# Five score banks as one tile, or as two tiles of two banks and one shared bank, with the exponential in two parts

## The chip, the cores and the metric

The kernel runs on one core of a Trainium2 chip. The engines of that core that matter here are TensorE (PE: matmuls and transposes, results in PSUM), VectorE (DVE: reductions, subtractions), ScalarE (ACT: exponentials and copies out of PSUM), GpSimd (POOL) and SyncE (SP), whose queue issues the DMAs. Each engine works off its own queue in order; semaphores hold an instruction until others are done. PSUM has eight banks of 512 fp32 values per partition. The metric is the device time of one execution in microseconds; less is better. "Before" is the median of three runs.

## What is computed

Attention over queries that are averaged two by two, then two expert layers:

```python
q_pool = q.reshape(B, H, S // factor, factor, D).mean(axis=3)      # 4 x 8 x 576 x 64
scores = scale * np.matmul(q_pool, k.transpose(0, 1, 3, 2))        # 576 x 1152 per head
scores = scores - np.max(scores, axis=-1, keepdims=True)
attn = np.exp(scores)
attn = attn / (np.sum(attn, axis=-1, keepdims=True) + 1e-09)
x = np.matmul(attn, v)                                             # then (B*S, H*D) = (2304, 512)
h = x @ w_in;  g = np.maximum(0.01 * h, h);  x = g @ w_out         # 512 -> 2048 -> 512
h = np.maximum(np.maximum(x @ w1, x @ w2), x @ w3); x = h @ w_out  # 512 -> 768 -> 512
```

## The kernel before

**Tiling.** The work goes by batches (4) and within a batch by pairs of heads (`NP` = 4), so by 16 pairs `n`. A pair's 576 queries per head are cut into tiles of 128 rows: five tiles in phase 0 (two of each head and one mixed tile "m" with 64 rows of each) and four in phase 1. A score tile is 128 queries by 1152 keys, in three chunks (`SC` = 3) of 384 keys (`SN`), each in a PSUM bank of its own. fp32 values are split into a high and a low part, so a chunk takes two matmuls (four for the mixed tile): six (twelve) for the tile.

**A score tile** (`scores`, L271 to L307): the matmuls, named `s` in the profile; the negated row maxima `mx` on DVE (L299 over the two banks that were filled first, L300 over the third, L301 the minimum of both); the exponential on ACT (L304) from all three banks to `p`, with the row sums as a second output. `normalise` (L309) turns a phase's sums into reciprocals.

**Banks.** In the first batch (`n < NP`) the tiles take turns in one PSUM tile of five banks, `five` (L91): one tile has banks 0, 1, 2 and the next 3, 4, 2, and bank 2, which both use, is filled last. The other three banks hold transposes and preparation (two, `ps_m`) and the value product (one). In the later batches there are three score banks, and the expert layers use the two that are freed.

**Order.** `attention` lays out slots, nine per phase. In each slot the probabilities of the current phase are transposed (`pst`, copied to `pt` by ACT at L344; `psf` and the DVE copy at L353 for the mixed tile), every third slot ends with the value matmuls (`pv`), and at given slots the scores of the next phase, the next pair's preparation (`psq`, `psk`, then L248, L213 on ACT and L252, L216 on DVE) and its loads are put in between. The first batch has no expert layer beside it. Instead eight chunks of expert weights are read from their 64-bit form (`wraw`, two buffers), decoded on DVE (L553 to L563), ACT and POOL, and stored. From the second batch on expert layers of the batch before run between the slots (`m`). A scheduler takes this order, the declared dependences and priorities (maxima and exponentials get a high one, `EARLY`) and makes each engine's queue of it; it also sets the semaphore waits.

All matmuls go through one helper, so they have one line, L108, and are told apart by tile.

Of the kernel before, what the change touches and what calls it, by code (L numbers as in the profile page):

```python
# [7 lines left out]
F32 = mybir.dt.float32  # L8
# [4 lines left out]
ACTF = mybir.ActivationFunctionType  # L13
ALU = mybir.AluOpType
AX = mybir.AxisListType
# [7 lines left out]
def kernel(  # L23
# [21 lines left out]
    nc = tc.nc  # L45
    B, H, S, D = q.shape
    T = S // 2
    NP = H // 2
# [7 lines left out]
    SC = 3  # L56
    SN = S // SC
# [16 lines left out]
    rr_p = ctx.enter_context(tc.tile_pool(name="rr", bufs=6))  # L74
# [13 lines left out]
    psum = ExitStack()  # L88
    ctx.callback(psum.close)
    ps_5 = psum.enter_context(tc.tile_pool(name="ps_5", bufs=1, space=bass.MemoryType.PSUM))  # L90
    five = ps_5.tile([128, 5, 512], F32, name="s5")  # L91

    ident = const.tile([128, 128], F32, name="ident")
    ebias = const.tile([128, 1], F32, name="ebias")
# [29 lines left out]
    def matmul(**kwargs):  # L124
        return on_pe(nc.tensor.matmul, **kwargs)
# [9 lines left out]
    def wide_scores():  # L135
        if not ps_w:
            psum.close()
            ps_s = ctx.enter_context(tc.tile_pool(name="ps_s", bufs=1, space=bass.MemoryType.PSUM))
            ps_w["s"] = ps_s.tile([128, SC, 512], F32, name="s")
            ps_w["m"] = ctx.enter_context(tc.tile_pool(name="ps_n", bufs=2, space=bass.MemoryType.PSUM))  # L140
        return ps_w["s"]
# [19 lines left out]
    def q_of(n):  # L161
        return spare if n < NP and n % 2 else qt
# [99 lines left out]
    def tiles_of(ph):  # L262
        if ph == 0:
            return [("a", 0), ("a", 128), ("b", 0), ("b", 128), ("m", X0 - 64)]
        return [(h, c) for h in "ab" for c in range(X0 + 64, T + 64, 128)]

    ptl = {}
    sums = {}
    flat = [0]

    def scores(n, ph, i):  # L271
        kind, c0 = tiles_of(ph)[i]
        parts = {"a": [0], "b": [1], "m": [0, 1]}[kind]
        steps = [(j, part) for j in parts for part in range(2)]
        if n < NP:
            ps = five[:, 2 * flat[0]:2 * flat[0] + SC]
            order = [1, 2, 0] if flat[0] else [0, 1, 2]
            flat[0] = 1 - flat[0]
        else:
            ps = wide_scores()  # L280
            order = [0, 1, 2]
        for c in order:
            for x, (j, part) in enumerate(steps):
                matmul(
                    out=ps[:, c, 0:SN],
                    lhsT=q_of(n)[j, part][:, c0:c0 + 128],
                    rhs=kts[n][j][:, c * SN:(c + 1) * SN],
                    start=(x == 0),
                    stop=(x == len(steps) - 1),
                )  # L290
        mx = st_p.tile([128, 4], F32, tag="st", name="mx")
        p = p_p.tile([128, SC, SN], F32, tag="p", name="p")
        if (n, ph) not in sums:
            sums[n, ph] = rr_p.tile([128, 8], F32, tag="rr", name="sums")
        rs = sums[n, ph]
        with tc.high_priority(offset=EARLY):
            if n < NP:
                first = ps[:, order[0]:order[0] + 2, 0:SN]
                nc.vector.tensor_reduce(out=mx[:, 1:2], in_=first, axis=AX.XY, op=ALU.max, negate=True)  # L299
                nc.vector.tensor_reduce(out=mx[:, 2:3], in_=ps[:, order[2], 0:SN], axis=AX.X, op=ALU.max, negate=True)  # L300
                nc.vector.tensor_reduce(out=mx[:, 0:1], in_=mx[:, 1:3], axis=AX.X, op=ALU.min)  # L301
            else:
                nc.vector.tensor_reduce(out=mx[:, 0:1], in_=ps[:, :, 0:SN], axis=AX.XY, op=ALU.max, negate=True)  # L303
            nc.scalar.activation(  # L304
                out=p, in_=ps[:, :, 0:SN], func=ACTF.Exp, bias=mx[:, 0:1], accum_out=rs[:, i:i + 1]
            )
        ptl[n, ph, i] = p  # L307

    def normalise(n, ph, i):  # L309
        rs = sums[n, ph]  # L310
        c = slice(i, i + 1)
        if n < FREE:
            if i < len(tiles_of(ph)) - 1:
                return
            c = slice(0, i + 1)
        nc.vector.tensor_scalar(out=rs[:, c], in0=rs[:, c], scalar1=1e-9, scalar2=None, op0=ALU.add)
        nc.vector.reciprocal(out=rs[:, c], in_=rs[:, c])
        if n >= FREE or i == 4:
            p = ptl[n, ph, i]
            nc.vector.tensor_scalar(out=p, in0=p, scalar1=rs[:, i:i + 1], scalar2=None, op0=ALU.mult)  # L320
# [91 lines left out]
    def attention():  # L412
        npair = B * NP
        load_pair(0)
        for j in range(2):
            pool_q(0, j, j + 1)
            prep_q(0, j)
            prep_k(0, j)
            if j == 0:
                for i in range(2):  # L420
                    scores(0, 0, i)
                    normalise(0, 0, i)
# [3 lines left out]
        for i in range(2, 5):  # L426
            scores(0, 0, i)
            normalise(0, 0, i)
# [212 lines left out]
    class Main:  # L641
        n = TM
# [11 lines left out]
    class Rest:  # L654
        n = TR_
# [102 lines left out]
    if True:  # L758
        nc.gpsimd.memset(ident, 0.0)
        nc.gpsimd.affine_select(  # L760
            out=ident, in_=ident, pattern=[[-1, 128]], compare_op=ALU.not_equal, fill=1.0, base=0, channel_multiplier=1
# [73 lines left out]
```

## Time and profile before

| | |
|---|---|
| median of three runs | 1422.62 us (1419.65 to 1423.52) |
| the profiled execution | 1429.25 us, span 1427.5 us |
| PE busy | 1284.6 us, 90% of the span |
| DVE, ACT, POOL busy | 714.9, 628.1, 360.3 us |
| chain that ended last | PE 73%, DVE 12%, ACT 5%, DMA 5%, issue 4% |
| first expert matmul | 261.58 us after the start |

The page gives the busy share of each engine in 40 slices, the chain of work that ended last and the costliest groups of instructions. Other views of the same trace are used below: waits (who waited for whom), a timeline (instructions in order of time), groups by shape, and a table of busy time by stage. Times are microseconds from the start of the span unless marked ns. Busy time says how long an engine worked, not whether anything waited for it; that is read from the idle time in square brackets and what ended it.

### The profile page before, as it was taken

Reading aid. Unit: us, or ns where it says so; the run is one execution under the profiler, and the core shown is the slowest. Engines: PE = TensorE matmul, PEld = TensorE weight load, DVE = VectorE, ACT = ScalarE, POOL = GpSimd, SP = SyncE. Lnnn points to the kernel's source line nnn. Section 1 sums busy time; section 2 is a strip of 40 time slices with the busy share of each in tenths; the row PEclk is TensorE's granted clock in tenths of the full one; section 3 lists DMA queues with packets and bytes.
Section 4 is the critical chain, followed back from the end, with each engine's and each line's share of the span. In section 5 each row is a group of like instructions: output and inputs, shape, how many; then the busy total and the mean of one; then the engine's idle time right before and its main releaser. Section 6 shows DMA issues by size and latency. Waiting matters only on the chain.

```text
span 1427.5 us, 19289 instructions
## 1 busy us (share of the span) xinstructions
PE 1284.6 (90%) x7376; PEld 1029.8 (72%) x7376; DVE 714.9 (50%) x1206; ACT 628.1 (44%) x1181; POOL 360.3 (25%) x322
## 2 busy tenths in 40 slices
PE   3767777888988898999999998999999999999998
PEld 3545555666666676867777786777777778888888
DVE  4575444369778868444555544454545421122110
ACT  3556455455555656444444444353545432111111
POOL 1152011245557554212112111010221002223110
PEclk9888899999999999999999999999999999999999
DMA  3357203265565656435443535353533335443343
GB/s 107 82 192 218 53 18 70 64 191 175 191 213 186 208 175 209 155 121 146 131 146 129 148 122 142 129 162 108 168 123 122 106 107 176 133 131 121 118 133 104
DMA packets 88056, 197.51 MB, mean 138 GB/s; under 512 B 11420, under 2 KB 41884, under 8 KB 87964
## 3 DMA queue, kind: packets, MB, share of 16 engines
q1 hardware_dynamic: 87964, 196.28, 44.1%
q8 instruction: 58, 0.95, 0.3%
q14 instruction: 34, 0.28, 0.1%
HBM read 150.99 MB, written 35.13 MB: 130 GB/s over the span
## 4 chain that ended last, share of the span: by engine, by line
PE 73%; DVE 12%; ACT 5%; DMA 5%; issue 4%; POOL 2%; SPq 0%; DVEq 0%; ACTq 0%; POOLq 0%
PE m L108 38%; PE s L108 11%; PE pv L108 10%; PE pst L108 6%; PE o L108 5%; ACT p L304 2%; DVE mx L303 2%; DMA wraw<-in_moe_w_out_dram 2%; DVE wraw L556 2%; DVE mx L299 1%; DVE wmant L553 1%; DMA qraw<-in_q_dram 1%; DVE q L252 1%; POOL wmant L566 1%; DVE pt L353 1%
## 5 line engine op out<-in xcount | busy, mean ns | idle before, releaser
L108 PE MATMUL m<-x,w 128*128 128x512 f32 x1272 | 320.8, 397 | 0.0
L108 PEld LDWEIGHTS m<-x,w 128*128 128x128 f32 x1272 | 231.3, 188 | 55.6 <-issue 13.5
L344 ACT COPY pt<-pst 128x512 f32<-128x512 f32 x288 | 166.5, 586 | 196.0 <-PE pst L108 194.7
L304 ACT ACTIVATE p<-s,mx 128x1152 f32<-128x1152 f32 x144 | 176.3, 1224 | 141.5 <-DVE mx L303 91.6
L108 PE MATMUL s<-kt,q 128*128 128x384 f32 x840 | 191.2, 363 | 43.5 <-ACT p L304 39.3
L303 DVE TENSOR_REDUCE mx<-s 128x1 f32<-128x1152 f32 x108 | 146.3, 1355 | 123.7 <-PE s L108 121.4
L108 PE MATMUL pv<-pt,v 128*64 128x256 f32 (+1 forms) x1152 | 183.6, 459 | 19.0 <-DVE pt L353 16.5
L108 PE MATMUL pst<-ident,p 128*128 128x128 f32 x1152 | 177.4, 279 | 20.3 <-DVE pt L353 8.9
L108 PEld LDWEIGHTS s<-kt,q 128*128 128x128 f32 x840 | 152.0, 199 | 55.7 <-ACT p L304 46.0
L108 PEld LDWEIGHTS pst<-ident,p 128*128 128x128 f32 x1152 | 140.6, 143 | 57.9 <-issue 10.9
L701 POOL TENSOR_TENSOR g<-t,g 128x512 fp32r<-128x512 f32 x64 | 83.8, 1309 | 347.8 <-DVE g L700 347.8
L108 PE MATMUL m<-g,w 128*128 128x512 f32 x624 | 163.0, 400 | 0.0
L108 PEld LDWEIGHTS pv<-pt,v 128*64 128x64 f32 x1152 | 81.6, 151 | 90.2 <-issue 34.1
L108 PEld LDWEIGHTS m<-g,w 128*128 128x128 f32 x624 | 112.0, 188 | 26.7 <-issue 7.2
L699 ACT ACTIVATE t<-m 128x512 f32<-128x512 f32 x80 | 44.3, 555 | 131.6 <-PE m L108 131.6
L108 PE MATMUL m<-x,wsplit 128*128 128x512 f32 x360 | 98.3, 413 | 0.5 <-ACT pt L344 0.4
L700 DVE CAST g<-t 128x512 fp32r<-128x512 f32 x64 | 31.4, 490 | 111.1 <-ACT t L699 110.6
L566 POOL TENSOR_TENSOR wmant<-wraw 128x512 f32<-128x512 f32 x56 | 63.6, 1137 | 91.9 <-DVE wraw L563 83.2
L580 POOL TENSOR_TENSOR wsplit<-wmant,wsplit 128x512 fp32r<-128x512 f32 x56 | 77.0, 1378 | 35.4 <-ACT wsplit L579 34.2
L639 POOL TENSOR_TENSOR y<-t,y 128x512 fp32r<-128x512 f32 x24 | 31.1, 1296 | 201.7 <-ACT y L638 201.7
L108 PEld LDWEIGHTS m<-x,wsplit 128*128 128x128 f32 x360 | 67.1, 195 | 19.6 <-issue 5.7
L729 DVE TENSOR_TENSOR t<-m,t 128x512 f32<-128x512 f32 (+1 forms) x60 | 38.2, 637 | 83.2 <-PE m L108 72.3
(87 smaller groups left out, 1491.9 us busy)
## 6 DMA issues: line engine op xcount, KB each, us to landing
w<-w SPq DMA_DIRECT2D x176, 512.0 KB, 3.4
w<-wsplit SPq DMA_DIRECT2D x56, 512.0 KB, 3.2
wraw<-in_moe_w_out_dram SPq DMA_DIRECT2D x22, 512.0 KB, 5.8
v<-in_v_dram SPq DMA_DIRECT2D x16, 576.0 KB, 3.8
wraw<-in_moe_w_dram SPq DMA_DIRECT2D x18, 512.0 KB, 5.4
qraw<-in_q_dram SPq DMA_DIRECT2D x15, 576.0 KB
kraw<-in_k_dram SPq DMA_DIRECT2D x15, 576.0 KB, 6.8
q<-q SPq DMA_DIRECT2D x52, 160.0 KB, 3.3
```

Of the source, the lines that this page charges most:

```text
L108: mm = f(*args, **kwargs)
L303: nc.vector.tensor_reduce(out=mx[:, 0:1], in_=ps[:, :, 0:SN], axis=AX.XY, op=ALU.max, negate=True)
L304: nc.scalar.activation(out=p, in_=ps[:, :, 0:SN], func=ACTF.Exp, bias=mx[:, 0:1], accum_out=rs[:, i:i + 1])
L344: nc.scalar.copy(out=dst, in_=ps.rearrange("p (j c) -> p j c", j=2))
L556: nc.vector.scalar_tensor_tensor(out=low.bitcast(F32), in0=low.bitcast(U32), scalar=2.0 ** -32, in1=m, op0=ALU.mult, op1=ALU.add)
L566: nc.gpsimd.tensor_tensor(out=mf, in0=low.bitcast(F32), in1=high.bitcast(F32), op=ALU.mult)
L580: nc.gpsimd.tensor_tensor(out=t[:, 1], in0=r, in1=t[:, 0], op=ALU.subtract)
L639: nc.gpsimd.tensor_tensor(out=t[:, 1], in0=src, in1=t[:, 0], op=ALU.subtract)
L699: nc.scalar.activation(out=t, in_=ps[:, 0:k.n], func=ACTF.Prelu, alpha=0.01)
L700: nc.vector.tensor_copy(out=gt[:, 0], in_=t)
L701: nc.gpsimd.tensor_tensor(out=gt[:, 1], in0=t, in1=gt[:, 0], op=ALU.subtract)
L729: nc.vector.tensor_tensor(out=t, in0=ps[:, 0:k.n], in1=t, op=ALU.max)
```

## The change

The tile `five` becomes two tiles of two banks, `s_pair`, and one tile of one bank, `s_mid`. A score tile puts its first two chunks into one of the pairs, in turn, and its third chunk into `s_mid`. The first maximum (L299) is taken over the pair, the second (L300) over `s_mid`. The exponential is two instructions: first the third chunk from `s_mid`, then the two chunks of the pair; each has a sum of its own (columns 8 and up of `sums`, which grows from 8 to 16 columns, and columns 0 and up), and `normalise` adds them with one more DVE instruction per phase. Later batches are as before.

```diff
-    five = ps_5.tile([128, 5, 512], F32, name="s5")
+    s_pair = [ps_5.tile([128, 2, 512], F32, name=f"s2{i}") for i in range(2)]
+    s_mid = ps_5.tile([128, 512], F32, name="s1")
...
         if n < NP:
-            ps = five[:, 2 * flat[0]:2 * flat[0] + SC]
-            order = [1, 2, 0] if flat[0] else [0, 1, 2]
+            two = s_pair[flat[0]]
             flat[0] = 1 - flat[0]
+            banks = [two[:, 0], two[:, 1], s_mid]
         else:
             ps = wide_scores()
-            order = [0, 1, 2]
-        for c in order:
+            banks = [ps[:, c] for c in range(SC)]
+        for c in range(SC):
...
-                    out=ps[:, c, 0:SN],
+                    out=banks[c][:, 0:SN],
...
             if n < NP:
-                first = ps[:, order[0]:order[0] + 2, 0:SN]
-                nc.vector.tensor_reduce(out=mx[:, 1:2], in_=first, axis=AX.XY, op=ALU.max, negate=True)
-                nc.vector.tensor_reduce(out=mx[:, 2:3], in_=ps[:, order[2], 0:SN], axis=AX.X, op=ALU.max, negate=True)
+                nc.vector.tensor_reduce(out=mx[:, 1:2], in_=two[:, :, 0:SN], axis=AX.XY, op=ALU.max, negate=True)
+                nc.vector.tensor_reduce(out=mx[:, 2:3], in_=s_mid[:, 0:SN], axis=AX.X, op=ALU.max, negate=True)
                 nc.vector.tensor_reduce(out=mx[:, 0:1], in_=mx[:, 1:3], axis=AX.X, op=ALU.min)
+                nc.scalar.activation(
+                    out=p[:, 2], in_=s_mid[:, 0:SN], func=ACTF.Exp, bias=mx[:, 0:1], accum_out=rs[:, 8 + i:9 + i]
+                )
+                nc.scalar.activation(
+                    out=p[:, 0:2], in_=two[:, :, 0:SN], func=ACTF.Exp, bias=mx[:, 0:1], accum_out=rs[:, i:i + 1]
+                )
...
+        if n < NP:
+            nc.vector.tensor_tensor(out=rs[:, c], in0=rs[:, c], in1=rs[:, 8:9 + i], op=ALU.add)
```

The scheduler makes other queues of this for the first batch; behind it every engine's order is the same. Three places show what moves. In the rows a tile's name has its number, and in brackets stand the engines or DMA queues that the instruction waits for. `s5_117` is the tile of five banks; `s20_117`, `s21_118` and `s1_119` are the two pairs and the shared bank.

TensorE at the start, the scores of the second and third tile of the program, before:

```order
L108 MATMUL s5_117<-kt0_204,q00_122 128x384 [waits Activation_49]
L108 MATMUL s5_117<-kt0_204,q01_123 128x384
L108 MATMUL s5_117<-kt0_204,q00_122 128x384
L108 MATMUL s5_117<-kt0_204,q01_123 128x384
L108 MATMUL s5_117<-kt0_204,q00_122 128x384
L108 MATMUL s5_117<-kt0_204,q01_123 128x384
L108 MATMUL pst_357<-ident_118,p_244 128x128 [waits DVE_49,PE_49]
L108 MATMUL pst_376<-ident_118,p_244 128x128 [waits DVE_49]
L108 MATMUL s5_117<-kt1_205,q10_124 128x384 [waits Activation_49]
L108 MATMUL s5_117<-kt1_205,q11_125 128x384
```

The wait of the first of six matmuls is for the exponential of the tile before, also at the second tile, whose first bank that exponential doesn't read. All six stand behind it.

TensorE in the first batch, the scores of the third pair's first tiles, while the second pair's values are worked on (a value product, transposes, the spread reciprocals `psr`), after:

```order
L109 MATMUL s20_117<-kt1_803,q10_126 128x384 [waits DMAHW2_49]
L109 MATMUL s20_117<-kt1_803,q11_127 128x384 [waits DMAHW4_49]
L109 MATMUL s20_117<-kt1_803,q10_126 128x384
L109 MATMUL s20_117<-kt1_803,q11_127 128x384
L109 MATMUL psr_1102<-ident_120,mb_1100 128x128 [waits Activation_49,Pool_49]
L109 MATMUL psr_1102<-ident_120,mb_1100 128x128
L109 MATMUL s1_119<-kt1_803,q10_126 128x384 [waits Activation_49]
L109 MATMUL s1_119<-kt1_803,q11_127 128x384
L109 MATMUL s21_118<-kt1_803,q10_126 128x384 [waits Activation_49]
L109 MATMUL s21_118<-kt1_803,q11_127 128x384
L109 MATMUL s21_118<-kt1_803,q10_126 128x384
L109 MATMUL s21_118<-kt1_803,q11_127 128x384
```

The same place before:

```order
L108 MATMUL psr_1075<-ident_118,mb_1073 128x128 [waits Activation_49,Pool_49]
L108 MATMUL psr_1075<-ident_118,mb_1073 128x128
L108 MATMUL s5_117<-kt1_783,q10_124 128x384 [waits DMAHW6_49,Activation_49]
L108 MATMUL s5_117<-kt1_783,q11_125 128x384 [waits DMAHW1_49]
L108 MATMUL s5_117<-kt1_783,q10_124 128x384
L108 MATMUL s5_117<-kt1_783,q11_125 128x384
L108 MATMUL s5_117<-kt1_783,q10_124 128x384
L108 MATMUL s5_117<-kt1_783,q11_125 128x384
```

The pair of a tile now stands ahead of its shared bank by itself, without a wait for ACT or with one for a tile further back, and `s1_119` waits for the first part of the exponential before it.

DVE at the same place, the maxima of four tiles after (L323 is the added sum of `normalise`):

```order
L299 TENSOR_REDUCE mx_1093<-s20_117 128x1 [waits PE_49,Activation_49]
L300 TENSOR_REDUCE mx_1093<-s1_119 128x1 [waits PE_49]
L299 TENSOR_REDUCE mx_1125<-s21_118 128x1 [waits PE_49,Activation_49]
L301 TENSOR_REDUCE mx_1093<-mx_1093 128x1 [waits DVE_49]
L300 TENSOR_REDUCE mx_1125<-s1_119 128x1 [waits PE_49]
L301 TENSOR_REDUCE mx_1125<-mx_1125 128x1 [waits DVE_49]
L299 TENSOR_REDUCE mx_1156<-s20_117 128x1 [waits PE_49,Activation_49]
L300 TENSOR_REDUCE mx_1156<-s1_119 128x1 [waits PE_49]
L299 TENSOR_REDUCE mx_1186<-s21_118 128x1 [waits PE_49,Activation_49]
L301 TENSOR_REDUCE mx_1156<-mx_1156 128x1 [waits DVE_49]
```

Before, three rows of a tile stand together, and the second has no wait of its own:

```order
L299 TENSOR_REDUCE mx_1022<-s5_117 128x1 [waits PE_49,Activation_49]
L300 TENSOR_REDUCE mx_1022<-s5_117 128x1
L301 TENSOR_REDUCE mx_1022<-mx_1022 128x1 [waits DVE_49]
L299 TENSOR_REDUCE mx_1067<-s5_117 128x1 [waits PE_49,Activation_49]
L300 TENSOR_REDUCE mx_1067<-s5_117 128x1
L301 TENSOR_REDUCE mx_1067<-mx_1067 128x1 [waits DVE_49]
```

The next tile's maximum over its pair has moved ahead of this tile's minimum (L301) at two of the places, and the maximum over the shared bank waits for TensorE by itself.

## Rows read from the trace of the kernel before

**Rows 1.** The page's part 2: busy tenths of PE in 40 slices.
```profile
PE   3767777888988898999999998999999999999998
```
**Rows 2.** The timeline: start us, length us, engine, instruction, [idle before <-releaser].
```profile
261.58 2.78 PE L108 MATMUL m<-x,w 128*128 128x512 f32 x11
```
**Rows 3.** Waits from 14 to 240 us: who for whom, us, times, longest.
```profile
PE s L108 <- ACT p L304: 41.6, 24, 4.0
PE psf L108 <- ACT pt L344: 5.2, 5, 2.1
```
**Rows 4.** The timeline of one tile's ring, 141 to 146 us.
```profile
141.54 1.22 ACT L304 ACTIVATE p<-s,mx 128x1152 f32<-128x1152 f32 x1 [0.64 <-DVE mx L301]
...
142.75 0.57 ACT L344 COPY pt<-pst 128x512 f32<-128x512 f32 x1
142.90 1.31 PE L108 MATMUL s<-kt,q 128*128 128x384 f32 x6 [0.43 <-ACT p L304]
...
144.32 0.96 DVE L299 TENSOR_REDUCE mx<-s 128x1 f32<-128x768 f32 x1 [2.81 <-PE s L108]
...
145.19 0.55 DVE L300 TENSOR_REDUCE mx<-s 128x1 f32<-128x384 f32 x1
145.78 0.15 DVE L301 TENSOR_REDUCE mx<-mx 128x1 f32<-128x2 f32 x1
145.97 1.22 ACT L304 ACTIVATE p<-s,mx 128x1152 f32<-128x1152 f32 x1 [0.20 <-DVE mx L301]
```
**Rows 5.** The timeline of the start.
```profile
24.60 2.29 PE L108 MATMUL s<-kt,q 128*128 128x384 f32 x6 [2.69 <-ACT p L304]
26.69 0.63 PE L108 MATMUL pst<-ident,p 128*128 128x128 f32 x2
...
30.07 2.29 PE L108 MATMUL s<-kt,q 128*128 128x384 f32 x6 [2.75 <-ACT p L304]
...
52.90 2.50 PE L108 MATMUL pv<-pt,v 128*64 128x320 f32 x12
```
**Rows 6.** Groups by shape, 14 to 240 us: xcount, busy us, mean ns, idle before.
```profile
L304 ACT ACTIVATE p<-s,mx 128x1152 f32<-128x1152 f32 x36 | 44.0, 1223 | 48.8 <-DVE mx L301 48.8
...
L344 ACT COPY pt<-pst 128x512 f32<-128x512 f32 x63 | 35.9, 585 | 42.0 <-PE pst L108 41.8
...
L304 ACT ACTIVATION_READ_ACCUMULATOR p<-s,mx 128x1 f32 x36 | 7.0, 195 | 0.0
...
L330 ACT COPY rb<-psr 128x256 f32<-128x256 f32 x7 | 2.6, 375 | 0.2
```
**Rows 7.** Busy time by stage: stretch, length, engines, PEclk, DMA share, GB/s.
```profile
11.00:52.90 41.90, 24.63 (x91) 20.50 (x91) 20.81 (x44) 17.18 (x34) 3.45 (x3) 0.94 0.18 43
52.90:109.00 56.10, 39.88 (x205) 26.83 (x205) 39.15 (x78) 31.91 (x58) 23.25 (x20) 0.84 0.58 178
...
140.20:159.50 19.30, 13.24 (x81) 10.21 (x80) 7.19 (x15) 9.21 (x16) 0.96 (x2) 0.93 0.00 1
159.50:194.00 34.50, 27.11 (x158) 18.54 (x157) 16.91 (x37) 18.84 (x38) 4.44 (x5) 0.84 0.30 73
```
**Rows 8.** The timeline of a decode round.
```profile
81.01 2.05 SPq L543 DMA_DIRECT2D wraw<-in_moe_w_out_dram  x2
...
85.27 0.61 DVE L553 TENSOR_SCALAR wmant<-wraw 128x512 int32<-128x512 int32 x1 [0.61 <-DMA wraw<-in_moe_w_out_dram]
...
87.35 1.41 PE L108 MATMUL s<-kspare,qspare 128*128 128x384 f32 x6 [3.78 <-ACT p L304]
...
90.40 2.32 SPq L543 DMA_DIRECT2D wraw<-in_moe_w_out_dram  x2
```
**Rows 9.** The timeline where a pair is prepared.
```profile
171.41 0.74 PE L108 MATMUL psq<-ident,qraw 72*128 72x72 f32 x4 [1.90 <-ACT pt L344]
...
172.29 3.47 PE L108 MATMUL pv<-pt,v 128*64 128x320 f32 x12
...
183.60 1.83 PE L108 MATMUL pv<-pt,v 128*64 128x320 f32 x12
```

More of the change, by code (lines that the diff above doesn't have):

```diff
@@ L293, in scores @@
         if (n, ph) not in sums:
-            sums[n, ph] = rr_p.tile([128, 8], F32, tag="rr", name="sums")
+            sums[n, ph] = rr_p.tile([128, 16], F32, tag="rr", name="sums")
         rs = sums[n, ph]
@@ L297, in scores @@
             if n < NP:
-                first = ps[:, order[0]:order[0] + 2, 0:SN]
-                nc.vector.tensor_reduce(out=mx[:, 1:2], in_=first, axis=AX.XY, op=ALU.max, negate=True)
-                nc.vector.tensor_reduce(out=mx[:, 2:3], in_=ps[:, order[2], 0:SN], axis=AX.X, op=ALU.max, negate=True)
+                nc.vector.tensor_reduce(out=mx[:, 1:2], in_=two[:, :, 0:SN], axis=AX.XY, op=ALU.max, negate=True)
+                nc.vector.tensor_reduce(out=mx[:, 2:3], in_=s_mid[:, 0:SN], axis=AX.X, op=ALU.max, negate=True)
                 nc.vector.tensor_reduce(out=mx[:, 0:1], in_=mx[:, 1:3], axis=AX.X, op=ALU.min)
+                nc.scalar.activation(
[4 more added lines that the diff above has]
+                )
             else:
                 nc.vector.tensor_reduce(out=mx[:, 0:1], in_=ps[:, :, 0:SN], axis=AX.XY, op=ALU.max, negate=True)
-            nc.scalar.activation(
-                out=p, in_=ps[:, :, 0:SN], func=ACTF.Exp, bias=mx[:, 0:1], accum_out=rs[:, i:i + 1]
-            )
+                nc.scalar.activation(
+                    out=p, in_=ps[:, :, 0:SN], func=ACTF.Exp, bias=mx[:, 0:1], accum_out=rs[:, i:i + 1]
+                )
         ptl[n, ph, i] = p
```

## Prediction

> **What bounds the kernel now.** I read the slices of the page first, then the table of waits for the stretch before the first expert matmul, then the timeline of one score tile in it, and last the stage table. The slices show where TensorE is not full [rows 1]: its first eight slices of 35.7 us, up to about 285 us, lie at 3 to 8 tenths, and after that it is nearly solid. The expert layers of the first batch begin at 261.58 us [rows 2]; until then attention runs alone, and whatever shortens that stretch shortens the kernel, since everything behind it is TensorE work queued in the same order in both kernels.
>
> The waits of that stretch have one large row [rows 3]: the score matmuls wait 24 times and 41.6 us for the exponential. The next ones are 5 us and less.
>
> The timeline of one tile says why [rows 4]. The exponential of a tile starts at 141.54 and ends at 142.76; at 142.90 TensorE starts all six matmuls of the next tile, DVE starts its maxima only at 144.32, when all six are done, takes 0.96, 0.55 and 0.15 us, and the next exponential starts at 145.97. That is a ring of 4.43 us in which nothing overlaps, although the two tiles share only one of five banks. The order of the program agrees (first listing of the section on the change): the first of the six carries a wait for ACT, also where it writes a bank of its own. So the five banks of `five` buy nothing now: the dependence is drawn on the whole tile. At the start, where the same six matmuls take 2.29 instead of 1.31 us, the ring is 30.07 − 24.60 = 5.47 us [rows 5].
>
> **Part 1: three tiles in place of one.** The waits in the order move as the diff says. In the second listing the pair of the tile carries no wait for the exponential just ahead of it, and the shared bank waits for that one's first part. So TensorE can fill two banks of the next tile under the maxima and the exponential of this one, and DVE can reduce them there too.
>
> What is left of the ring is the shared bank: short exponential, two matmuls, reduction, minimum. The price of the short exponential comes from two copies of the same engine: 375 ns for 256 elements, 585 ns for 512 [rows 6], so 0.82 ns per element and for the exponential 1223 − 1152 × 0.82 = 0.28 us fixed. For 384 elements that is 0.59 us, for 768 it is 0.91 us. The new ring is then 0.59 + 0.14 (end of the exponential to the matmul, as at 142.76 to 142.90) + two of six matmuls, 0.44, + 0.11 to DVE + 0.59 (start of L300 to start of L301) + 0.19 = 2.06 us in place of 4.43 [rows 4]. It gives up to 2.4 us per tile where TensorE has nothing else to do; where it has, the wait shown is the limit. So I price it by stage, each ended by whatever comes next.
>
> *Start, to the first value matmul at 52.90 us.* TensorE is idle 41.90 − 24.63 = 17.3 us of this stage [rows 7]. With the ring shortened, a tile costs TensorE 2.09 us for six matmuls (24.60 to 26.69) and 0.63 us for two transposes [rows 5], 2.72 us in all, which is more than the ring (2.06 plus some 0.3 for slower matmuls): TensorE itself comes next. The ring is run four times (tiles two to five) and once at the tile with twelve matmuls: 4 × (5.47 − 2.72) = 11 us, and 1 us at the fifth. I take −12 us; bounds −8 (a third of it stays as waits on the query preparation) and −15 (nearly all of the idle time goes).
>
> *Decoding, 52.90 to 109 us.* Here the exponential is not the only thing late: the next pair of weight chunks is fetched at 81.01 us, DVE stands in its queue at the first decode instruction until that fetch lands at 85.27, the maximum behind it follows, and the score matmuls get going at 87.35 after 3.78 us [rows 8]. This wait stays: the fetches are paced by two buffers (81.01 to 90.40 is 9.4 us per pair) and not by the scores. Five rounds need at least some 4 × 9.4 = 38 us where the stage now has 56 us with 39.88 busy on TensorE [rows 7]. So up to 16 us could go and, if the maxima happen to stand behind more fetches than now, something can come back. I take −6; bounds −11 and +2.
>
> *The two later stretches that score a pair's first five tiles* (140.2 to 159.5 us, and the same one pair later). TensorE idles 19.30 − 13.24 = 6.06 us there, all of it for the exponential [rows 7]. I went through the changed order by hand with the durations of [rows 4]. Two waits remain, about 1.5 and 1.8 us, because DVE reduces the next tile's pair (0.96 us) ahead of this tile's minimum (third listing): the gain from running ahead is paid back in part there. So 6.06 − 3.3 = 2.8 us, and 1 us more if one group of six runs at the rate of [rows 4] in place of that of [rows 5] (the clock of this stage is 0.93 now [rows 7]). −4 each, −8 together; bounds −4 and −12.
>
> *The other stretches*, which prepare the next pair. Their waits hang on query preparation through ACT (1.90 us ahead of 171.41, then value matmuls that take 3.47 us in place of 1.8 [rows 9]), and the change puts a little more on ACT there. I take −1 in all, bounds +3 and −5.
>
> **Part 2: the exponential in two, and its sums.** 36 tiles have it (nine per pair, four pairs). The second instruction costs its fixed part, 0.28 us; the read of the sum is hidden, since 1.21 us after an exponential starts the next instruction starts [rows 4]. So ACT gains 36 × 0.28 = 10 us of work; if each read were exposed too, at its own 195 ns [rows 6], it is 17 us. Nothing can be below zero, the same elements are worked on. In the stretch from 140.2 ACT is busy 9.21 of 19.30 us [rows 7]; with 5 × 0.28 = 1.4 more and 15.3 us left it is at 10.6 of 15.3. So it is hidden under TensorE, save that each copy of transposes behind a split exponential starts 0.28 later: this is what I have counted against the other stretches. The eight added sums of columns (one per phase) are like L301, 0.15 us [rows 4], 1.2 us on DVE, which waits anyway; the cover gone, 1.2 us.
>
> The fixed part, 0.28 us, is from [rows 6]. The Trainium skill, ScalarE: Activation LUTs, section What ACT_TABLE_LOAD costs, states some 280 ns plus 0.833 ns per element for an activation whose bias is a pointer, as here, and an overlap of 93 ns between two in a row. By that the split costs 36 × 0.19 = 7 us of ACT in place of 10; the rows agree on the fixed part and don't show the overlap.
>
> **Sum.** −12 −6 −8 −1 = −27 us against the profiled execution, 1429.25 us: 1402. That execution lies 6.6 us above the median, 1422.62; the same difference gives **1396 us**. Behind 261.58 us the order of every engine is the same as before, so I let the gain pass through whole.
>
> **Rivals.**
> 1. *Other waits take over* (decoding and query preparation). For it: in the decoding stage DVE waits in its queue, and in the other stretches ACT is the releaser. Then only the start (−10) and half of the later stretches (−4) are left and +4 comes back: −10, **1413 us**. Chance 0.15.
> 2. *Nearly all of it goes, and the matmuls speed up too.* The granted clock is 0.84 in the stages from 52.9 and 159.5 [rows 7], between its two levels, 1.2 and 2.4 GHz; the slow six matmuls come behind waits. If the waits go and the clock stays high, 41.6 us less about 8 that remain, and some 8 us of matmul time: −42, **1381 us**. Against it: value matmuls are slow at 172.29 behind a wait that the change leaves alone [rows 9]. Chance 0.13.
> 3. *ACT becomes the bound, slower than before.* Place: the stretches that score five tiles and copy transposes. If an exponential in two parts costs 17 us in all and the copies of transposes behind it release TensorE later in each step, so that the 41.6 us move to rows now at 5 us [rows 3], the time is 1423 + 17 = **1440 us**. It decides from 27 / 36 = 0.75 us of exposed cost per tile, against 0.28 by the rows. Chance 0.03. The Trainium skill, Perfetto Trace Analysis, section Optimizing Scalar/DVE Operations, advises larger instructions where the engine is saturated; ACT, at 48% in the stretch from 140.2, is not.
> 4. *The waits are gone from the order but the queue holds them elsewhere*: on TensorE the matmul of the shared bank waits where the pair waited, and work behind it stands as long. Against it: that wait ends 0.64 us after the exponential starts, not 1.36. Within 3 us of **1423 us**. Chance 0.07.
>
> **How the numbers follow.** Forecast 0.62, rivals 0.15, 0.13, 0.03 and 0.07. About 0.3% is what a measurement of this kernel can tell from no change: 4.3 us. Faster by more: 0.62 + 0.15 + 0.13, less a little for rival 1 falling short, 0.88; within: 0.08; slower: 0.04. The bounds of the stages add up to −43 at one end and −7 at the other; the range of 8 in 10 is **1382 to 1412 us**: it takes in the forecast's own range (1389 to 1408), and half of rivals 1 and 2.
>
> **What the profile after would show.** The wait of the scores for the exponential falls from 41.6 us to 15 or less, on the shared bank alone. First value matmul near 41 us (right) or after 47 (wrong). First expert matmul near 235 us. The five-tile stretch 15 to 16 us instead of 19.3, with waits of 1.5 to 2 us ahead of the shared bank. The split exponential 0.59 and 0.91 us, 36 each. If the decode fetches stay 9 to 15 us apart and the stage stays at 56 us, the −6 was wrong; if waits on the copies of transposes grow past 25 us, rival 3's mechanism is at work, and I would be wrong on the cover.

## The result, and the profile after

The changed kernel takes **1400.84 us** (median of four runs, 1397.46 to 1402.59) where the kernel before takes 1422.03 (four runs, 1419.65 to 1423.52): ratio 0.985, interval 0.9825 to 0.9874. In a second group of runs it took 1400.28 against 1423.85, ratio 0.9832 (0.9809 to 0.9855). The forecast was 1396 us, range 1382 to 1412. The profiled execution has a span of 1400.8 us; that of the kernel before had 1427.5. Here and below, one of the ten executions of split_only, 1843.42 us at a granted clock of 0.645, is left out of its median as slow.

The busy tenths and TensorE's clock in 40 slices of 35.0 us, after (compare [rows 1]):

```profile
PE   5778879798898988999999998999999999999998
...
PEclk8889889998998999999999999999999999999999
```

The first seven slices, up to 245 us, read 5 to 9 where the first eight, up to 285 us, read 3 to 8. The waits up to 240 us, after (compare [rows 3]):

```profile
PE s L109 <- ACT p L302: 21.1, 15, 3.3
...
PE pst L109 <- ACT pt L352: 5.2, 7, 2.3
...
PE psf L109 <- ACT pt L352: 5.0, 4, 1.7
...
PE psq L109 <- ACT pt L352: 4.6, 3, 2.0
```

The wait for the exponential is half of what it was, 21.1 for 41.6 us, and it is for L302, the short part; the long part, L305, is waited for 0.4 us. The row itself differs between executions: it is 24.2 us in the second profile of the same kernel (after_again). The waits on ACT's copies are 14.8 us in these three rows.

The ring after, from the timeline of the first five-tile stretch (compare [rows 4]):

```profile
127.23 0.55 DVE L300 TENSOR_REDUCE mx<-s 128x1 f32<-128x384 f32 x1
...
127.70 0.95 DVE L299 TENSOR_REDUCE mx<-s 128x1 f32<-128x768 f32 x1
128.00 1.08 ACT L352 COPY pt<-pst 128x512 f32<-128x512 f32 x2 [1.12 <-PE pst L109]
128.56 0.14 DVE L301 TENSOR_REDUCE mx<-mx 128x1 f32<-128x2 f32 x1
128.97 0.59 ACT L302 ACTIVATE p<-s,mx 128x384 f32<-128x384 f32 x1
...
129.54 0.90 ACT L305 ACTIVATE p<-s,mx 128x768 f32<-128x768 f32 x1
...
129.70 0.62 PE L109 MATMUL s<-kt,q 128*128 128x384 f32 x2 [1.30 <-ACT p L302]
...
131.14 0.58 ACT L302 ACTIVATE p<-s,mx 128x384 f32<-128x384 f32 x1 [0.61 <-DVE mx L301]
```

From one short exponential to the next it is 131.14 − 128.97 = 2.17 us; it was 4.43. Only two matmuls of the next tile stand behind the short part, and DVE takes the next tile's pair at 127.70, before this tile's minimum at 128.56: that is the running ahead. Busy time by stage, after (stretch, length, then PE, PEld, DVE, ACT and POOL busy, granted clock of TensorE, DMA share, GB/s; compare [rows 7]):

```profile
11.00:41.21 30.21, 21.54 (x91) 16.94 (x91) 21.41 (x46) 19.68 (x49) 3.46 (x3) 0.80 0.24 60
41.21:83.27 42.06, 33.73 (x190) 22.77 (x189) 29.31 (x59) 28.45 (x63) 15.99 (x15) 0.86 0.56 174
...
83.27:123.45 40.18, 29.31 (x156) 18.56 (x155) 28.50 (x58) 24.65 (x57) 15.50 (x14) 0.79 0.75 246
...
123.45:138.00 14.55, 11.80 (x81) 9.37 (x80) 5.93 (x12) 9.84 (x23) 0.07 (x1) 1.00 0.00 1
```

The third row in the kernel before, between the same value products:

```profile
105.42:140.15 34.73, 26.67 (x156) 17.98 (x155) 21.36 (x45) 20.55 (x41) 10.08 (x10) 0.85 0.77 232
```

And the first expert matmul, after (compare [rows 2]):

```profile
234.76 3.69 PE L109 MATMUL m<-x,w 128*128 128x512 f32 x15
```

It comes 26.8 us earlier; from there to the end it is 1166.0 us, near the 1165.9 of the kernel before in these two profiles.

Stage lengths in us of the kernels below, all from their timelines, cut at the same value products (the 1st, 6th, 10th, 12th, 16th and 18th, from zero to the first expert matmul):

| kernel | to 1st | to 6th | to 10th | to 12th | to 16th | to 18th | to expert | sum | behind it |
|---|---|---|---|---|---|---|---|---|---|
| before | 52.9 | 52.5 | 34.7 | 19.4 | 34.5 | 19.4 | 48.2 | 261.6 | 1165.9 |
| before_again | 52.9 | 54.0 | 35.1 | 19.4 | 34.5 | 19.4 | 48.2 | 263.5 | 1156.4 |
| after | 41.2 | 42.1 | 40.2 | 14.6 | 32.5 | 14.6 | 49.7 | 234.8 | 1166.0 |
| after_again | 40.9 | 43.3 | 39.9 | 14.6 | 32.4 | 14.6 | 49.2 | 234.8 | 1162.9 |
| split_only | 56.6 | 53.1 | 35.8 | 19.4 | 34.4 | 21.2 | 51.7 | 272.0 | 1162.3 |
| small_mid | 40.6 | 44.1 | 37.5 | 14.8 | 32.8 | 14.8 | 49.4 | 234.0 | 1156.2 |
| small_mid_min | 42.8 | 42.8 | 40.9 | 12.6 | 34.7 | 12.6 | 49.7 | 236.1 | 1157.8 |
| pair_first | 50.6 | 46.7 | 37.4 | 16.3 | 35.4 | 16.6 | 51.4 | 254.4 | 1160.2 |
| min_first | 40.7 | 43.6 | 37.1 | 13.1 | 33.9 | 13.0 | 50.0 | 231.4 | 1164.0 |
| min_first_pad | 40.8 | 45.3 | 40.2 | 13.0 | 34.5 | 13.1 | 50.8 | 237.7 | 1160.7 |
| apart_min | 42.9 | 43.3 | 38.5 | 13.1 | 34.3 | 13.1 | 50.0 | 235.1 | 1157.9 |
| act_extra | 40.7 | 40.5 | 40.1 | 14.6 | 32.9 | 14.6 | 49.0 | 232.4 | 1163.1 |
| before_nopre | 52.5 | 51.3 | 32.6 | 18.4 | 32.8 | 18.5 | 48.1 | 254.0 | 1162.3 |
| after_nopre | 40.2 | 43.1 | 34.0 | 14.9 | 33.7 | 14.6 | 49.0 | 229.4 | 1162.7 |

### The profile page after: what moved, and what is told of

The parts are those of the page before. It is cut to its first block, busy times and chain, and to the rows that moved or that the text cites. A ratio compares the mean times of both kernels' runs of the same rounds, so it can differ in the third digit from the quotient of the medians.

```text
span 1400.8 us, 19351 instructions
## 1 busy us (share of the span) xinstructions
PE 1282.2 (92%) x7376; PEld 1025.2 (73%) x7376; DVE 711.9 (51%) x1214; ACT 637.1 (45%) x1253; POOL 362.2 (26%) x322
## 4 chain that ended last, share of the span: by engine, by line
PE 70%; DVE 11%; DMA 6%; ACT 5%; issue 4%; POOL 4%; SPq 0%; POOLq 0%; DVEq 0%; ACTq 0%
PE m L109 38%; PE pv L109 10%; PE s L109 9%; PE pst L109 6%; PE o L109 5%; DMA wraw<-in_moe_w_out_dram 3%; DVE mx L309 2%; POOL wmant L574 2%; DMA qraw<-in_q_dram 1%; DVE wraw L564 1%; DMA wraw<-in_moe_w_in_dram 1%; POOL wsplit L588 1%; DVE wmant L561 1%; DVE wmant L567 1%; DVE q L253 1%
## 5 line engine op out<-in xcount | busy, mean ns | idle before, releaser
L109 PE MATMUL s<-kt,q 128*128 128x384 f32 x840 | 189.9, 360 | 31.3 <-ACT p L310 14.9
L310 ACT ACTIVATE p<-s,mx 128x1152 f32<-128x1152 f32 x108 | 132.3, 1225 | 89.1 <-DVE mx L309 88.3
L588 POOL TENSOR_TENSOR wsplit<-wmant,wsplit 128x512 fp32r<-128x512 f32 x56 | 77.3, 1384 | 35.1 <-ACT wsplit L587 35.1
```

What stands on the lines that cost most here:

```text
L109: mm = f(*args, **kwargs)
L310: nc.scalar.activation(out=p, in_=ps[:, :, 0:SN], func=ACTF.Exp, bias=mx[:, 0:1], accum_out=rs[:, i:i + 1])
L588: nc.gpsimd.tensor_tensor(out=t[:, 1], in0=r, in1=t[:, 0], op=ALU.subtract)
```

## Experiments

### Is it the dependence, or the split? (split_only)

The changed kernel with the five banks as one tile again; the exponential and its sums stay in two parts:

```diff
-    s_pair = [ps_5.tile([128, 2, 512], F32, name=f"s2{i}") for i in range(2)]
-    s_mid = ps_5.tile([128, 512], F32, name="s1")
+    five = ps_5.tile([128, 5, 512], F32, name="s5")
+    s_pair = [five[:, 0:2], five[:, 3:5]]
+    s_mid = five[:, 2]
```

> The five banks stay one tile; only the exponential and its sums are split in two, shared bank first. Theory (the gain comes from the dependence on the tile alone): the first score matmul still waits for everything that reads the tile, now 0.59 + 0.90 us of exponential in place of 1.22, so the ring grows from 4.43 to some 4.7 us and 24 waits by 0.28 us each: the wait of the scores for the exponential 48 us in place of 41.6, the time 1422 + 7 = 1429 us. Rival (the split itself brings the gain, since the shared bank comes free early): 1401 to 1410 us. Second rival (ACT's added work is covered everywhere): 1422 us.

Measured: 1432.26 us (nine runs) against 1424.31, ratio 1.0062 (1.0038 to 1.0086), 8 to 9 us slower than before. Its ring, from the timeline:

```profile
146.79 0.58 ACT L303 ACTIVATE p<-s,mx 128x384 f32<-128x384 f32 x1 [0.64 <-DVE mx L302]
...
147.36 0.89 ACT L306 ACTIVATE p<-s,mx 128x768 f32<-128x768 f32 x1
...
148.40 1.33 PE L110 MATMUL s<-kt,q 128*128 128x384 f32 x6 [0.67 <-ACT p L306]
...
151.47 0.58 ACT L303 ACTIVATE p<-s,mx 128x384 f32<-128x384 f32 x1 [0.20 <-DVE mx L302]
```

All six matmuls start at 148.40, behind the long part, and the ring is 4.68 us. The short part frees nothing: the split alone costs, and without tiles of their own there is no gain at all. The row of waits was 43.1 us and not 48; the rest of the loss shows up in the stage lengths, above all at the start (56.6 for 52.9) and in the last stage (51.7 for 48.2).

### Is the ring over the shared bank what is left? (pair_first)

The two exponentials of the changed kernel in the other order:

```diff
+                nc.scalar.activation(out=p[:, 0:2], in_=two[:, :, 0:SN], ...)
                 nc.scalar.activation(out=p[:, 2], in_=s_mid[:, 0:SN], ...)
-                nc.scalar.activation(out=p[:, 0:2], in_=two[:, :, 0:SN], ...)
```

> Three tiles as in the changed kernel, but the exponential over the pair first and over the shared bank second. Theory (what is left in the changed kernel is the ring over the shared bank): the ring grows by the long part, 0.90 us, from 2.06 to some 2.96 us; the 15 waits, 21.1 us, for the shared bank's exponential in the changed kernel's trace grow by up to 0.9 us each, 13 us, and a few new ones come: 1414 us (1408 to 1418). Rival (what is left are copies, maxima and transfers, and the order of the two parts plays no role): 1401 us, within 3.

Measured: 1417.0 us, ratio 0.996 (0.994 to 0.998). The waits up to 240 us:

```profile
PE s L109 <- ACT p L305: 24.0, 11, 3.7
...
PE s L109 <- ACT p L302: 6.1, 4, 1.9
...
PE psf L109 <- DVE mx L301: 3.9, 1, 3.9
```

The scores wait 30.1 us for 21.1, and the first expert matmul stands at 254.4. In its first five-tile stretch the long parts start at 140.28 and 143.33, a ring of 3.05 us. So the order of the two parts carries some 16 of the 21 to 24 us, about half of it at the start, where the first value product falls back from 41 to 50.6 us. The time was inside what I expected (1408 to 1418); the waits of the scores grew by 9 us where I had 13, and part of the rest lies in waits that I had not listed, such as the 3.9 us of `psf` for a maximum.

### The running ahead of DVE (min_first)

The changed kernel with one more rule of order (no wait is added, both are on DVE):

```diff
-                nc.vector.tensor_reduce(out=mx[:, 1:2], in_=two[:, :, 0:SN], ...)
+                red = nc.vector.tensor_reduce(out=mx[:, 1:2], in_=two[:, :, 0:SN], ...)
...
-                nc.vector.tensor_reduce(out=mx[:, 0:1], in_=mx[:, 1:3], axis=AX.X, op=ALU.min)
+                if low[0] is not None:
+                    tc.add_manual_dep(red.ins, low[0].name, NOSYNC, reason="minimum first")
+                low[0] = nc.vector.tensor_reduce(out=mx[:, 0:1], in_=mx[:, 1:3], axis=AX.X, op=ALU.min).ins
```

> The changed kernel with one more rule of order: a tile's minimum (0.15 us) stands in DVE's queue ahead of the next tile's maximum over its pair (0.96 us); nine such pairs stand the other way round in the changed kernel. Theory (in the stretches of five tiles the running ahead of DVE is paid back): the two waits of 1.30 and 1.45 us in such a stretch lose about 0.9 us each; over four stretches and the start 6 to 8 us: 1394 us (1391 to 1398). Rival (ACT's copies of transposes stand ahead of the exponential there, so an earlier minimum releases nothing, and the later maximum delays the next tile): 1401 us, within 3.

Measured: 1396.41 us, ratio 0.9807 (0.978 to 0.9833). Its stages from the 10th to the 16th value product, and the waits:

```profile
121.44:134.50 13.06, 11.84 (x82) 9.37 (x81) 6.26 (x12) 9.52 (x23) 0.09 (x1) 1.00 0.00 1
134.50:168.43 33.93, 27.04 (x157) 18.15 (x156) 18.29 (x42) 20.61 (x51) 5.37 (x6) 0.85 0.30 74
```

```profile
PE s L109 <- ACT p L305: 9.8, 9, 3.2
```

The two waits ahead of the shared bank in its first five-tile stretch:

```profile
127.21 0.62 PE L109 MATMUL s<-kt,q 128*128 128x384 f32 x2 [0.81 <-ACT p L305]
...
133.95 0.62 PE L109 MATMUL s<-kt,q 128*128 128x384 f32 x2 [0.41 <-ACT p L305]
```

The place was right: these two were 1.30 and 1.45 us, all the waits for the short part fall from 21.1 to 9.8 us, and a five-tile stretch from 14.6 to 13.05. But the stretch behind it takes 33.9 us in place of 32.5. Three profiles with this order (min_first, min_first_pad, apart_min) have the first expert matmul at 231.4, 237.7 and 235.1; the changed kernel has it twice at 234.8. So the stretch of query preparation takes back most of what the five-tile stretch ahead of it gives, and the times (0.9807 against 0.9832, intervals that overlap) don't settle a gain.

### A smaller shared bank (small_mid and small_mid_min)

```diff
+        cuts = [0, 512, 1024, S] if n < NP else [0, SN, 2 * SN, S]
...
-                    rhs=kts[n][j][:, c * SN:(c + 1) * SN],
+                    rhs=kts[n][j][:, cuts[c]:cuts[c + 1]],
```

with the maxima and the exponentials over the same cuts; small_mid_min has the order of min_first too.

> The changed kernel with other cuts: the pair takes keys 0 to 1023 (two banks full of 512) and the shared bank the last 128, in place of three times 384. The ring over the shared bank gets shorter: short exponential 0.28 + 128 x 0.82 ns = 0.39 us for 0.59, its maximum some 0.28 for 0.55, its two matmuls some 0.2 for 0.44: 1.3 us in place of 2.06, while the pair's maximum, which DVE runs ahead of the minimum, grows from 0.96 to some 1.23. Theory (where DVE runs ahead, the waits are set by the pair's maximum and not by the ring): the gains and the loss nearly cancel, 1398 us (1395 to 1401). Rival (the ring over the shared bank is what is left): 15 waits shorter by 0.76 us, 1390 us.

> Both the cuts at 512 and 1024 and the minimum ahead of the next tile's maximum. Theory (the ring over the shared bank still sets the 9 waits, 9.8 us, that are left with the minimum first): most of these go, 4 to 7 us less than with the order alone, 1391 us (1388 to 1394). Rival (with the minimum first, copies, query preparation and the matmuls' own time set the stretch): 1396 us, within 2.5; or above it, if the longer maximum of 1.23 us no longer fits under the ring.

Measured: 1398.9 us, ratio 0.9822 (0.9798 to 0.9846), and 1397.25, ratio 0.9819 (0.9793 to 0.9845). The waits for the short exponential fell to 14.2 and 10.1 us and no time came of it: first expert matmul at 234.0 and 236.1. The first expectation held. In the second the rival held: the waits are no shorter than with the order alone (10.1 against 9.8 us), the five-tile stretch gains 0.4 to 0.5 us and other stages lose it, and my theory there fell.

### Is ACT's added work covered? (act_extra)

```diff
+                nc.scalar.activation(
+                    out=idle, in_=mx[:, 0:1], func=ACTF.Exp, bias=mx[:, 0:1]
+                )
```

> The changed kernel with one more instruction on ACT behind each split exponential: an exponential of one element per row into a tile that nobody reads, by its fixed part some 0.28 us, 36 times, 10 us of ACT. That doubles what the split costs on ACT. Theory (ACT's added work is covered by TensorE, save where copies of transposes come behind it): 1400 to 1403 us, the waits on copies of transposes up by no more than 4 us. Rival (ACT is at its bound in the first batch): 10 us more, 1410 us.

Measured: 1396.39 us, ratio 0.9812 (0.9782 to 0.9843). The groups on ACT, 14 to 240 us:

```profile
L306 ACT ACTIVATE p<-s,mx 128x768 f32<-128x768 f32 x36 | 32.3, 897 | 0.0
L303 ACT ACTIVATE p<-s,mx 128x384 f32<-128x384 f32 x36 | 21.0, 585 | 12.3 <-DVE mx L302 11.9
L309 ACT ACTIVATE idle<-mx 128x1 f32<-128x1 f32 x36 | 10.6, 293 | 0.0
```

10.6 us of added work on ACT cost nothing that can be measured. The median is even 4 us lower; the interval overlaps that of the changed kernel (0.9809 to 0.9855), 2.4 us of it stand ahead of the first expert matmul, and the scheduler made a slightly different order of it, so this is not explained. The five-tile stretches are 14.6 us in both. ACT is not the bound.

### Decoding (after_nopre and before_nopre)

Both kernels with PRE = 0 in place of 8: the expert weights are decoded only when they are needed.

> The changed kernel without the eight early chunks of expert weights: they are decoded when the expert layers need them, so the first batch holds attention alone. To be compared with before_nopre of the same group. Theory (decoding is not what limits the gain; the scores' ring is): the two kernels without early decoding stand as far apart as those with it, 23 to 28 us. Rival (the fetches and DVE's decoding held a part of the gain back, as the first rival of the prediction says): they stand 32 us apart or more, since the first pair's second phase then gains what the start gains.

> The kernel before without the eight early chunks, the partner of after_nopre. In itself either way is possible: the first batch loses the decoding work (some 5 to 10 us shorter), and the first expert layer has eight chunks more to decode (DVE and POOL work that may hold TensorE up). What counts is the distance between the two: 23 to 28 us by the theory, 32 or more by the rival.

Measured: 1393.71 us (ratio 0.9798, 0.9767 to 0.9829) and 1420.82 us (0.9987, 0.9963 to 1.001). The distance is 27.1 us, as the theory has it (23 to 28), where the rival had 32 or more. The stage from the 1st to the 6th value product gains 8.2 us without early decoding and 10.5 with it, so decoding did not hold that gain back. It shows one stage later: from the 6th to the 10th the changed kernel loses 5.4 us with early decoding (40.2 for 34.7) and 1.4 without (34.0 for 32.6). Ahead of the first expert matmul the two kernels without early decoding stand 24.6 us apart, 2.5 less than in the time, so traces and medians agree to a few us and no better.

### The excess of the first profile (before_again) and the repeat (after_again)

> The kernel before, unchanged, profiled a second time, because its first profiled execution was 6.6 us above the median. Theory (the excess lies in the first batch, the rest of the program being work that always takes the same): first expert matmul at about 256 us in place of 261.58, and 1166 us behind it. Rival (the excess lies behind it): first expert matmul at 261 to 262 us again and some 1160 us behind it, so that the gain of 26.8 us ahead of it is real and something is given back later.

> The changed kernel, unchanged, timed in more rounds and profiled again. Theory (the gain sits in the first batch alone, and the rest of the program takes 1156 to 1166 us in either kernel): first expert matmul within 2 us of 234.76, and a gain over the kernel before of 24 us, near the 26.8 us of the two traces. Rival (part of the gain is given back behind the first batch): a gain of 21 us again, 1400 to 1403 us.

Measured: the second profile of the kernel before took 1421.65 us; the repeat of the changed kernel is given at the top. The stretch behind the first expert matmul, of both:

```profile
263.50:1419.90 1156.40, 1097.43 (x6381) 896.07 (x6378) 578.36 (x938) 491.34 (x921) 312.40 (x261) 0.98 0.46 148
```

```profile
234.80:1397.70 1162.90, 1102.84 (x6381) 900.58 (x6378) 577.85 (x938) 491.57 (x921) 312.09 (x261) 0.98 0.45 147
```

For before_again the theory fell: its first batch is no shorter than the first time (263.5 against 261.6), and the excess lay behind it, 1165.9 against 1156.4 us. For the repeat the place of the gain held (234.8 again), and 23.6 us of it arrived, nearer to the theory's 24 than to the rival's 21; but the interval, 0.9809 to 0.9855 or 20.6 to 27.2 us, holds both, and the time of 1400.28 us is one that the rival named.

### The slower matmuls of 256 columns (min_first_pad and apart_min)

All kernels with the wider sums show some groups of the last expert stage slower, so two kernels, both with the order of min_first, ask for the place of the tiles in SBUF. min_first_pad adds 64 bytes among the constants; apart_min leaves the sums at 8 columns and puts the short exponential's sums behind all other tiles:

```diff
+    rx_p = ctx.enter_context(tc.tile_pool(name="rx", bufs=6))
...
-            sums[n, ph] = rr_p.tile([128, 16], F32, tag="rr", name="sums")
+            sums[n, ph] = rr_p.tile([128, 8], F32, tag="rr", name="sums")
+            if n < NP:
+                short[n, ph] = rx_p.tile([128, 8], F32, tag="rx", name="short")
```

> The minimum first, and 64 bytes per partition more among the constants (with one memset at the start). The sums grew from 32 to 64 bytes in six buffers, so all tiles behind them stand 192 bytes further back in SBUF; with the 64 bytes it is 256. In all four kernels with the wider sums the matmuls of 256 columns in the last stage are slower: 283 ns for 276 (o from w and grest, 72) and 283 for 281 (m from x1rest, 216), some 1.7 us over the program. Theory (the place in SBUF sets it): the row of o from w and grest returns to 276 ns; the time 1.7 us less than with the order alone, which the times hardly resolve. Rival (something else in the queue sets it): the row stays at 283 ns.

> The minimum first, as in min_first, and the sums of the short exponential in a tile of their own behind all other tiles of SBUF, so that the sums keep their 32 bytes per buffer and every other tile stands where it stands in the kernel before. Theory (the last 600 us take 2 to 3 us more in every kernel with the wider sums because tiles moved in SBUF): the matmuls of o from w and grest return from 283 to 276 ns and those of m from x1rest from 283 to 281, the time is 2 us below min_first: 1394.5 us. Rival (it has another cause, such as the code): both rows stay at 283 ns, 1396 to 1398 us.

Measured: 1398.4 us (ratio 0.982, 0.9798 to 0.9843) and 1391.68 us (0.9783, 0.9751 to 0.9815). The groups from 270 us on (count, busy us, mean ns), first of after, then of apart_min:

```profile
L109 PE MATMUL m<-x1rest,w 128*128 128x256 f32 x216 | 26.9, 283 | 0.0
...
L109 PE MATMUL o<-w,grest 128*128 128x256 f32 x72 | 9.0, 283 | 0.0
```

```profile
L110 PE MATMUL m<-x1rest,w 128*128 128x256 f32 x216 | 26.4, 281 | 0.0
...
L110 PE MATMUL o<-w,grest 128*128 128x256 f32 x72 | 8.5, 276 | 0.0
```

With the 64 bytes the rows stay at 283 ns; with the old places they are back at 281 and 276, the values of the kernel before. So the rows go with where tiles stand in SBUF, as worked out from the order of the pools (no trace gives an address), and a shift of 256 bytes is no better than one of 192; why is not shown. Over the four groups of this kind it is 1.7 us. apart_min has the lowest median of all kernels here, but of its 4.7 us below min_first this explains only 1.7, and the two intervals overlap.

## Why the prediction was right, and where it was off

**The bound and the mechanism** were right. The wait for the whole tile was the ring of 4.43 us; with the dependence back (split_only) the ring is 4.68 and the gain is gone. The new ring was worked out as 2.06 us and is 2.17.

**Start, −12 us:** measured 52.9 − 41.2 = −11.7, the first value product at 41.21 for "near 41". It came about a little otherwise than worked out: TensorE idles 8.7 us in the stage in place of 17.3, which is 8.6 us, and its own 91 matmuls take 21.54 us in place of 24.63, while the sum had twelve of idle time and the matmuls at their slow rate. The granted clock of the stage does not tell why: it reads 0.80 after and 0.94 before, but 0.63 in the second profile of the kernel before, with the same length (52.9 us) and 25.46 us of matmuls.

**Decoding, −6 us, and the other stretches, −1:** the split between the two was off, their sum by 1.5 us. The stage to the 6th value product gained 10.5 us, at the good bound. One reason lies in [rows 8], where I took the 3.78 us ahead of the score matmuls for a wait on the fetch that stays. The maxima of that tile in the kernel before:

```profile
84.12 0.55 DVE L300 TENSOR_REDUCE mx<-s 128x1 f32<-128x384 f32 x1
...
85.81 0.14 DVE L301 TENSOR_REDUCE mx<-mx 128x1 f32<-128x2 f32 x1
```

The fetch and the decode instruction put the minimum off from 84.67 to 85.81, 1.1 us; the rest of the wait is the scores' ring, which the change shortens. After, the fetches of whole pairs are 9 to 14 us apart, as I said; the fourth pair is fetched in halves:

```profile
45.09 1.15 SPq L551 DMA_DIRECT2D wraw<-in_moe_w_in_dram  x2
...
57.32 2.10 SPq L551 DMA_DIRECT2D wraw<-in_moe_w_in_dram  x2
...
70.85 1.38 SPq L551 DMA_DIRECT2D wraw<-in_moe_w_out_dram  x2
...
80.17 0.38 SPq L551 DMA_DIRECT2D wraw<-in_moe_w_out_dram  x1
...
83.98 0.38 SPq L551 DMA_DIRECT2D wraw<-in_moe_w_out_dram  x1
```

and the ninth and tenth chunk in the kernel before:

```profile
103.06 0.38 SPq L543 DMA_DIRECT2D wraw<-in_moe_w_in_dram  x1
107.39 0.38 SPq L543 DMA_DIRECT2D wraw<-in_moe_w_in_dram  x1
```

The step that failed here is "Five rounds need at least some 4 × 9.4 = 38 us": the rounds need not end with the stage. By 83.27, the 6th value product, seven chunks are fetched; in the kernel before nine are by then (105.42). The others are decoded in the next stretch, which takes 5.4 us more. About half of that, 2.6 us, is TensorE's own time (29.31 for 26.67 us with 156 matmuls in both, at a granted clock of 0.79 for 0.85), the other half idle time. With the stretches from the 12th to the 16th product (−1.9) and from the 18th on (+1.5) the "other stretches" gave +5.0 in place of −1. Together with the −10.5 that is −5.5 us, where I had −7. That the two errors nearly cancel is in part the same decoding, moved by a stage, and in part luck: the later stretch was not priced for it. after_nopre and before_nopre show that the +5.4 comes mostly from decoding.

**The five-tile stretches, −4 each:** measured −4.8 each, with the two waits ahead of the shared bank at 1.30 and 1.45 us where 1.5 and 1.8 were worked out. The first is in the ring above, the second:

```profile
137.46 0.61 PE L109 MATMUL s<-kt,q 128*128 128x384 f32 x2 [1.45 <-ACT p L302]
```

That the running ahead of DVE makes more than half of them is shown by min_first (0.81 and 0.41 us are left, the stretch 13.05 us); that it costs the kernel something is not.

**ACT:** the two parts take 584 and 896 ns, 36 times each, for 1223 ns: 0.26 us more per tile, 9 us, for 10. It is covered, and so would be 10.6 us more (act_extra). The split starts its second part 0.57 us after the first and ends 1.47 us after it (128.97 to 130.44) against 1.22 before, so 0.25 us per tile is what the ring would see. The Trainium skill, ScalarE: Activation LUTs, section What ACT_TABLE_LOAD costs, has an overlap of 93 ns between two activations in a row, by which it would be 0.19; the trace shows 0.25. On the split as such, the Trainium skill, Perfetto Trace Analysis, section Optimizing Scalar/DVE Operations, says that breaking up instructions of an engine that isn't saturated but leaves others idle may let work end sooner. Here that holds only with the tiles apart: split_only has the same breaking up and is slower than before.

**The sum, −27 us, and what became of it behind 261 us.** Ahead of the first expert matmul the sum was right: 26.8 us, or 28.7 measured from before_again (263.5 − 234.8). In the medians 21 to 24 us arrive. So the step that was off is the last one, "I let the gain pass through whole"; it makes the miss of 4.8 us (1400.84 for 1396). To take the gain off the median, 6.6 us below the profiled execution, was no error: before_again shows that these 6.6 us lie behind the first batch, where the same work took 1165.9 and 1156.4 us. But that execution hid the loss. The two traces differ by the full 26.7 us, with 1165.9 and 1166.0 us behind, only because it was 7.2 us above its median (1422.03) and the changed kernel's profiled run, 1402.59, was 1.8 above its own.

An estimate follows if the scatter of a kernel lies behind its first expert matmul. Each profiled run's distance from the median of its group taken off, that stretch is 1158.7 and 1159.1 us in the two profiles of the kernel before, 1164.3 and 1163.7 in those of the changed one: some 5 us more. Of these 1.7 us are the slower matmuls of 256 columns. The rest stays open. The queues on TensorE are the same there in the twelve profiles with early decoding, but for a few rows in one, and still it takes 1156 to 1166 us; and not every kernel with the wider sums shows a loss (min_first_pad gains 25.5 us in the median and 23.9 to 25.8 ahead of the first expert matmul).

TensorE's own time is part of the gain too. Ahead of the first expert matmul, in the two profiles of the kernel before and then in the two of the changed one:

```profile
11.00:261.58 250.58, 179.21 (x989) 128.86 (x990) 131.31 (x263) 131.82 (x253) 45.80 (x43) 0.89 0.34 96
```

```profile
11.00:263.48 252.48, 182.36 (x989) 131.37 (x990) 131.91 (x262) 131.58 (x252) 45.42 (x43) 0.83 0.33 95
```

```profile
11.00:234.76 223.76, 174.49 (x989) 122.11 (x990) 132.05 (x270) 139.91 (x324) 45.88 (x43) 0.86 0.36 108
```

```profile
11.00:234.79 223.79, 171.16 (x990) 121.61 (x990) 131.79 (x270) 140.25 (x325) 45.95 (x43) 0.87 0.36 108
```

The same matmuls take 5 to 11 us less, for which the sum had 2 us; the idle time falls by 17 to 22.

**Signs and rivals.** The wait for the exponential was to be 15 us or less and is 21.1, 24.2 in the repeat; small_mid shows that a third less of it (14.2) brings no time that can be measured. First expert matmul 234.76 for "near 235", five-tile stretch 14.6 for 15 to 16. Rival 1 (1413) saw the pay-back through decoding but mis-sized it. Of rival 2 the faster matmuls came, 5 to 11 us for its 8, but half of the waits stayed and the clock did not stay high: 1.00 in the five-tile stretches, which had 0.93 and 0.91, but 0.79 from the 6th to the 10th value product, which had 0.85. Rival 3 is refuted by act_extra; the waits on copies grew from 10.4 to 14.8 us, not past 25. Rival 4 is refuted by the waits and the time. Its "0.64 us" from the start of the short exponential to the matmul did not fit the sum's own 0.59 + 0.14 = 0.73; the ring above shows 129.70 − 128.97 = 0.73.

## To carry to other kernels

When one tile spans banks that two generations of data use in turn, look in the order at which instruction carries the wait: a dependence on the whole tile can undo a double buffer that the layout already has, and tiles of their own give it back, here with the instruction that read all of it split over them. Where a ring remains over a shared part, put that part's reader first; here the order of the two parts was worth 16 us, the splitting alone cost 8 to 9. Two traces with an equal stretch behind the change don't show that a gain passes through whole: look how far each profiled run lies from its median, and take a second profile of each kernel.

## What was not expected of the hardware

The same matmuls of 128x256 (o from w and grest) take 276 ns or 283 ns, as far as these kernels tell by where their tiles stand in SBUF: widening a small tile ahead of them by 32 bytes in six buffers was enough, and 64 bytes more did not mend it. And the expert layers behind the first batch vary from one profiled execution to the next by up to 10 us, also between two profiles of one kernel (1165.9 and 1156.4 us); in the two profiles of the kernel before the granted clock of the second 145 us behind the first expert matmul is 0.94 and 0.98. The granted clock of the first stage, up to the first value product, reads 0.94 and 0.63 in these two profiles, and the stage is 52.9 us long in both.
